# Five small re-orderings in a fused top-k attention and low-rank mixer kernel: parameters, one scratch tile, shares of products, and when two pairs add u

## The chip, the cores and the metric

The kernel runs on one core of a Trainium2 chip. The metric is device time in microseconds (us) of one execution. The engines are named as the profile names them: PE is TensorE (PEld its weight loads), DVE is VectorE, ACT is ScalarE, POOL is GpSimd, SP is SyncE, which here only issues DMAs. A "q" after a name (SPq, ACTq) is that engine's sequencer issuing a DMA.

## The reference, cut to what matters

```python
# attention: q, k, v of (8, 8, 576, 64)
scores = q @ k.T / sqrt(64)
kth = the 32nd largest score of each row
scores = where(scores >= kth, scores, -1e9)
x = softmax(scores) @ v                 # (8, 576, 512) after the heads are put side by side
# mixer: U (576, 32), V (32, 576), w_ch1 (512, 2048), w_ch2 (2048, 512)
h = x.T @ U @ V
u = x + h.T
out = u + relu(u @ w_ch1) @ w_ch2
```

All parameters U, V, w_ch1, w_ch2 arrive as 64-bit floats and are turned into 32-bit floats on the chip.

## The kernel before, in words

**Pairs and steps.** Heads are worked on two at a time: 8 batches of 4 pairs, so 32 pairs (`g`), numbered 0 to 31; batch b holds pairs 4b to 4b+3. A pair has 576 query rows for each of its two heads: four main tiles (`t` 0 to 3, 128 rows, both heads) and one tail tile (`t` 4, the last 64 rows of both heads). Steps (`n`) follow each other in a loop written out by hand. In the first four pairs every tile has a step of its own (20 steps, n 0 to 19). From pair 4 on a pair has four steps, and its last step works on tile 3 and the tail together: three rows of work, which the code calls lanes 0, 1 and 2, lane 2 being the tail. Pair 4 is steps 20 to 23, pair 5 steps 24 to 27, pair 6 steps 28 to 31, and so on.

**One tile's way.** `scores` (L350, the tail's at L382) puts scores in PSUM, ACT copies them to SBUF (L395; the tail's L415 and L418). `front` finds the 32nd largest score on DVE, by four rounds of MAX8 (L521, L539) and MATCH_REPLACE8 (L534); the tail's rounds write a scratch row, `place`, in the only buffer of the tag "tplace". From pair 5 on the main tiles are first folded to half their width: POOL adds the halves (L446), DVE takes their maximum (L448) and POOL subtracts (L449); DVE then takes the best of the lower half (L502, L500). Then ACT makes a "gap" tile for each lane (`least` L565, E L568: zero where the score is among the 32), POOL subtracts it from the scores (L569), and ACT takes the exponential (L453). The gap tiles have the tag "E", which has two buffers; a step with three lanes needs three. Then the weights are transposed: by PE (L631, L636) with copies by ACT (L632, L637) up to pair 5; from pair 6 on by DVE (L595) and DMAs to DRAM and back. `values` (L705, L708, tail L679) multiplies with v three steps after the tile's own step, and ACT copies the product to XT (L717, L686).

**u.** When a pair's tail has its values, `mixed` is put in the list `mixing`. From pair 4 on it first lets `lag` shares pass, then POOL scales XT (L737, L740), PE transposes it (L747, L758), and after the next tile's values PE multiplies with U (L770) and V (L782), ACT copies (L797), and POOL adds to make u (L798). XT and `scale` have one buffer each, so a pair's u must be done with them before the next pair's are written.

**Products.** With u of a whole batch there, `mlp(b)` makes its products on PE: first layer L842, second layer L859, in two parts of 320 and 256 columns, 256 products a batch; L854 and L870 are ACT's evictions, L871 POOL's addition of u. They run beside the attention of the next batch: `fill` is called eight times a step, and each call advances `mixing` once and issues one share of products. A unit of work is 512 columns; a full share is 1.02 units, in a step with two tiles 1.4 times that. For steps up to 38 (`n <= ALONE + BATCH + 2`) the share is multiplied by EARLY = 0.91, in steps 24 to 27 by SECOND = 0.84. The products of batch b+1 may not pass the fourth quarter of the contraction before batch b+1 has all its u (`whole`): a `fill` that meets this gate issues nothing and drops what was due. The last batch's products (`closing`, L935) come after all attention.

**Parameters.** There are 36 pieces of parameters in a fixed order (U, V, 16 of w_ch1, 16 of w_ch2). `next_params(1)` does three stages at once, on three different pieces: it issues the DMA of the next on SP (L157); for the one issued by the call before it sets up three ACT passes (L179, L180, L183), which the following `fill` calls issue one each; and for the one before that it issues the join: a shift on DVE (L202, for the last eight pieces L193) and two additions on POOL (L203, L205). In steps of pairs 0 to 3 it is called at two places, from pair 4 on in the middle of a step (L1328, pair 4 alone) and at its end (L1354).

The order on each engine is the order in which the code issues; each engine works its queue in that order.

Of the kernel before, what the change touches and what calls it, by code (L numbers as in the profile page):

```python
# [8 lines left out]
F32 = mybir.dt.float32  # L9
# [17 lines left out]
def kernel(  # L27
# [29 lines left out]
    B, H, S, D = q.shape  # L57
    P = 128
# [4 lines left out]
    NT, TAIL = 4, 64  # L63
# [3 lines left out]
    NPAIR = H // 2  # L67
# [3 lines left out]
    ALONE = NPAIR * CH  # L71
# [11 lines left out]
    attn = ctx.enter_context(tc.tile_pool(name="attn", bufs=2))  # L83
# [63 lines left out]
    def f64_raw(srcs):  # L147


        n, w = srcs[0].shape[0], srcs[0].shape[-1]  # L150
        raw = mlpp.tile([P, 2 * C], U32, tag="raw", name="raw", bufs=3)
        if len(srcs[0].shape) == 3:
            raw = raw.rearrange("p (f w) -> p f w", w=w)
        else:
            raw = raw[:, 0:w]
        for i, src in enumerate(srcs):
            nc.sync.dma_start(raw[i * n : (i + 1) * n], src)  # L157
        return raw[0 : len(srcs) * n]

    def f64_parts(raw, out):  # L160

        n, w = raw.shape[0], raw.shape[-1] // 2
        d = "p f" if len(raw.shape) == 3 else "p"
        low, hi = (raw.rearrange(f"{d} (w two) -> {d} w two", two=2)[..., i] for i in range(2))
        low8 = raw.bitcast(U8).rearrange(f"{d} (w eight) -> {d} w eight", eight=8)[..., 3]
        if out is None:
            if not spare:  # L170

                uT = mlpp.tile([P, NC, S], F32, tag="uT", name="uT")
                words = uT.rearrange("p c n -> p (c n)").bitcast(U32)
                spare.extend(words[:, i * SLAB : (i + 1) * SLAB] for i in range(NT))
            out = spare.pop()[0:n, 0:w]
        bits = out.bitcast(U32)
        lows, his = low.bitcast(F32), hi.bitcast(F32)
        passes.extend((
            lambda: nc.scalar.activation(bits.bitcast(F32), his, AF.Copy, scale=RESCALE),  # L179
            lambda: nc.scalar.activation(  # L180
                lows, low8, AF.Identity, bias=four[0:n], scale=-(1 + 2.0**-10) * 2.0**-26
            ),
            lambda: nc.scalar.activation(his, his, AF.Sign, bias=nudge[0:n]),  # L183
        ))
        return hi, bits, low, len(params) < LATE

    def f64_join(hi, bits, low, late, outs):

        if late:
            none = nought if len(bits.shape) == 2 else nought.rearrange("p o -> p o ()")
            nc.vector.scalar_tensor_tensor(  # L193
                out=bits,
                in0=bits,
                scalar=3,
                in1=none.to_broadcast(list(bits.shape)),
                op0=ALU.logical_shift_left,
                op1=ALU.bitwise_or,
            )  # L200
        else:
            nc.vector.tensor_single_scalar(bits, bits, 3, ALU.logical_shift_left)  # L202
        nc.gpsimd.tensor_tensor(bits, bits, hi, ALU.add)  # L203
        for dst, form in outs:
            nc.gpsimd.tensor_tensor(dst.bitcast(U32), form(bits), form(low), ALU.add)  # L205
# [26 lines left out]
    def next_params(n):  # L232

        while passes:
            passes.pop(0)()
        while parts:
            f64_join(*parts.pop(0))
        while raws:
            r, outs = raws.pop(0)
            if isinstance(outs, list):  # L240
                parts.append((*f64_parts(r, None), outs))
                continue
            made = f64_parts(r, outs)
            parts.append((*made, [(made[1], same)]))
        for _ in range(min(n, len(params))):
            srcs, outs = params.pop()
            raws.append((f64_raw(srcs), outs))
# [6 lines left out]
    def load(g):  # L254

        list(loading(g))
# [211 lines left out]
    def front(tiles):  # L468
# [5 lines left out]
        for g, t in tiles:  # L474
# [4 lines left out]
            n = S2.shape[1]  # L479
# [61 lines left out]
        for c, chunk, total, _, way in lanes:  # L541
            if way == "pooled":
                gap = attn.tile([P, S], F32, tag="E", name="E")
# [17 lines left out]
        if gaps:  # L561
            slots = [lane[0] for lane in gaps]
            lo, hi = min(slots), max(slots) + 1
            least = small.tile([P, 3], F32, tag="least", name="least", bufs=3)
            nc.scalar.mul(least[:, lo:hi], m8[:, lo:hi, 7], WIDEN)  # L565
            for c, chunk, *_ in gaps:
                gap = attn.tile([P, S], F32, tag="E", name="E")
                nc.scalar.activation(gap, chunk, AF.Relu, bias=least[:, c : c + 1], scale=-WIDEN)  # L568
                nc.gpsimd.tensor_tensor(chunk, chunk, gap, ALU.subtract)  # L569
            yield  # L570
# [585 lines left out]
    STEPS = len(steps)  # L1156
    BATCH = NPAIR * NT


    SLOTS, LONG, EARLY, SECOND = 8, 1.4, 0.91, 0.84  # L1160
    share = MLP_WORK / (NPAIR * SLOTS * (NT - 1 + LONG))
    fillers, mixing, due = [], [], 0.0

    def fill(k=1):


        nonlocal due
        for _ in range(k):
            if passes:
                passes.pop(0)()  # L1170
            if mixing and next(mixing[0], True):
                mixing.pop(0)
            part = share * (LONG if len(tiles(n)) > 1 else 1)
            if n <= ALONE + BATCH + 2:
                part *= SECOND if ALONE + NT <= n < ALONE + 2 * NT else EARLY
            due += part
            while due > 0:
                if not fillers:
                    due = 0.0
                    break  # L1180
                done = next(fillers[0], None)
                if done is None:
                    fillers.pop(0)
                elif not done:
                    due = 0.0
                else:
                    due -= done

    def tiles(n):

        return steps[n] if 0 <= n < STEPS else []

    def weighted(m):

        for g, t in tiles(m):
            values(g, t)
        if tiles(m)[-1][1] == NT:
            mixing.append(mixed(g, None, 1) if m < STEPS - 1 else mixed(g, 5, 0))

    def turn():  # L1200

# [6 lines left out]
            yield from turns(g, t)  # L1208

    load(0)  # L1210
    next_params(3)
    t = 0
    for _ in prep(0):
        pass
# [3 lines left out]
    for n in range(STEPS + 2):  # L1218
        if n < STEPS:
            g, t = steps[n][0]  # L1220
            if t == 0 and g < NPAIR:
                load(g + 1)
            if t == (1 if g < NPAIR else 2) and g + 1 < NP:
                ready = prep(g + 1)
            fronts[n] = front(steps[n])
            next(fronts[n])
            if owed:
                inverse(owed.pop(), 0, 2 * NT + 1)
        else:
            t = NT  # L1230
        here, last = fronts.get(n, iter(())), fronts.pop(n - 1, iter(()))
        if n >= ALONE - 1 and n <= ALONE:
# [12 lines left out]
            if n < ALONE:  # L1245
                split(*steps[n + 1][0])
                next(here)
                next(here)
                inverse(g, 0, 2 * NT)
                mixing.append(mixed(g, 1))  # L1250
                fill()
                next(here)
                continue
            fill()
            scores(*steps[n + 1][0])
            fold(*steps[n + 1][0])
            next(here)
            while mixing:
                fill()
# [44 lines left out]
        if ALONE <= n - 3 <= STEPS - 3:  # L1304
            weighted(n - 3)
            if waiting:
                waiting.clear()
                if next(mixing[0], True):
                    mixing.pop(0)
# [14 lines left out]
        if n < STEPS and n - 2 >= ALONE and len(tiles(n - 2)) > 1:  # L1324
            scale(steps[n - 2][0][0])
        next(here, None)
        if g == NPAIR and t < NT - 1:
            next_params(1)  # L1328
        fill()
        if n >= STEPS:  # L1330
            if n == STEPS:
                inverse(NP - 1, 0, 2 * NT + 1)
                scale(NP - 1)
            weighted(n - 2)
# [15 lines left out]
                coming = loading(g + 2) if g + 2 < NP else iter(())  # L1350
            next(coming, None)
        next(ready, None)
        if t != 0 or g == NPAIR + 1:
            next_params(1)  # L1354
        next(here, None)
        fill()
# [36 lines left out]
```

## Time and profile before

| what | value |
|---|---|
| median of 3 runs | 1661.03 us (1660.91 to 1661.57) |
| the profiled execution's own time | 1660.23 us |
| its span, first to last instruction | 1658.0 us |
| mean granted TensorE clock | 0.968 |
| PE busy | 1555.6 us (94%) |
| DVE busy | 1546.9 us (93%) |
| ACT busy | 992.0 us (60%) |
| POOL busy | 1009.4 us (61%) |
| PE's idle waits between 190 and 1560 us, the longest | 7.25 us, at 259.28 |

The page of the profile gives busy shares in 40 slices of 41.5 us, and groups of instructions by line. The views by stretch of time (windows) give each engine's busy time in a stretch; the views of waits name who waited for whom; the timeline lists instructions with the idle time before them in square brackets and what ended it. A busy PE is not PE at its peak, as the ends of pipelined matmuls are modelled; a fp32 product shows as two matmul records.

### The profile page before, as it was taken

How to read it: one execution, taken by the hardware profiler on the slowest of the kernel's cores; microseconds unless marked ns; L12 is line 12 of the kernel's file. 1: busy time of each engine (PE TensorE's matmuls, PEld its weight loads, DVE VectorE, ACT ScalarE, POOL GpSimd, SP SyncE). 2: the span in 40 equal slices, each digit the busy share in tenths (PEclk: the TensorE clock that was granted, in tenths of full speed). 3: DMA queues.
4: the chain of work that ended last, by engine and by line, in shares of the span. 5: the costliest groups of instructions: out<-in, count | busy, mean ns of one | idle time of the engine just before them, and what ended most of it. 6: DMA issues, size and time to landing. Idle time of an engine off the chain costs nothing.

```text
span 1658.0 us, 30248 instructions
## 1 busy us (share of the span) xinstructions
PE 1555.6 (94%) x9638; PEld 1182.7 (71%) x9638; DVE 1546.9 (93%) x4394; ACT 992.0 (60%) x2475; POOL 1009.4 (61%) x881
## 2 busy tenths in 40 slices
PE   4566698999999999999999999999999999999999
PEld 2344466787677877788777877788777877787776
DVE  7999998999999999999999999999999999994452
ACT  5888886665655566566655656565655656564320
POOL 4888756666656565656656565656666565653620
PEclk7787799999999999999999999999999999999999
DMA  4333321254445555454545455454545455543001
GB/s 113 98 101 99 86 76 25 57 133 135 126 130 137 133 154 133 131 139 130 134 125 141 128 154 133 134 137 131 133 126 141 128 151 134 136 123 109 7 2 28
DMA packets 280399, 189.42 MB, mean 114 GB/s; under 512 B 174288, under 2 KB 261168, under 8 KB 280240
## 3 DMA queue, kind: packets, MB, share of 16 engines
q1 hardware_dynamic: 259728, 117.62, 29.4%
q10 hardware_dynamic: 20512, 69.87, 13.1%
q8 instruction: 76, 1.25, 0.3%
q14 instruction: 83, 0.68, 0.1%
HBM read 116.49 MB, written 70.91 MB: 113 GB/s over the span
## 4 chain that ended last, share of the span: by engine, by line
PE 74%; DVE 19%; DMA 2%; POOL 1%; ACT 1%; issue 1%; SPq 1%; ACTq 0%; DVEq 0%; POOLq 0%
PE mm L859 23%; PE mm L842 22%; PE sc L350 7%; DVE m L539 7%; PE O L708 6%; DVE upper L534 6%; PE mm L935 3%; DVE first L521 2%; PE sc L382 2%; PE sc L935 2%; PE tp L935 2%; PE up L782 2%; PE O L705 1%; PE tp L631 1%; DMA PT<-away 1%
## 5 line engine op out<-in xcount | busy, mean ns | idle before, releaser
L842 PE MATMUL mm<-uT,w 128*128 128x320 f32 (+1 forms) x1792 | 463.3, 410 | 2.2 <-POOL uT L798 2.2
L859 PE MATMUL mm<-hT,w 128*128 128x320 f32 (+1 forms) x1792 | 460.2, 407 | 0.0
L569 POOL TENSOR_TENSOR Ssb<-Ssb,E 128x576 f32<-128x576 f32 x243 | 339.7, 1418 | 187.0 <-ACT E L568 187.0
L842 PEld LDWEIGHTS mm<-uT,w 128*128 128x128 f32 x1792 | 334.6, 191 | 102.0 <-issue 7.4
L859 PEld LDWEIGHTS mm<-hT,w 128*128 128x128 f32 x1792 | 332.0, 190 | 92.6 <-issue 10.2
L539 DVE MAX8 m<-upper 128x8 f32<-128x304 f32 (+1 forms) x774 | 362.3, 508 | 0.7
L534 DVE MATCH_REPLACE8 upper<-m,upper 128x304 f32<-128x304 f32 (+1 forms) x516 | 256.5, 504 | 0.0
L449 POOL TENSOR_TENSOR lower<-lower,upper 128x576 uint32<-128x576 uint32 x108 | 152.3, 1410 | 135.9 <-DVE upper L448 133.7
L446 POOL TENSOR_TENSOR lower<-Ssb 128x576 uint32<-128x576 uint32 x108 | 152.3, 1410 | 133.4 <-ACT Ssb L395 73.5
L453 ACT ACTIVATE Ssb<-Ssb,nmax 128x576 f32<-128x576 f32 x258 | 201.8, 784 | 15.7 <-POOL Ssb L545 7.8
L350 PE MATMUL sc<-qkT 64*128 64x288 f32 (+1 forms) x1056 | 177.2, 457 | 13.9 <-ACT Ssb L404 12.2
L568 ACT ACTIVATE E<-Ssb,least 128x576 f32<-128x576 f32 x243 | 176.2, 769 | 4.2
L502 DVE MAX8 upper<-lower 128x8 f32<-128x288 f32 x432 | 171.7, 438 | 2.7 <-POOL lower L449 2.7
L395 ACT COPY Ssb<-sc 128x576 f32<-128x576 f32 x216 | 127.6, 644 | 68.3 <-PE sc L350 68.1
L595 DVE STREAM_TRANSPOSE y<-Ssb 128x512 f32<-128x512 f32 (+1 forms) x312 | 154.0, 543 | 1.2 <-ACT Ssb L453 1.2
L708 PE MATMUL O<-PT,va 128*64 128x128 f32 x2048 | 143.7, 284 | 0.0
L854 ACT ACTIVATE hT<-mm 128x320 f32<-128x320 f32 (+1 forms) x224 | 91.2, 407 | 81.7 <-PE mm L842 78.7
L350 PEld LDWEIGHTS sc<-qkT 64*128 64x128 f32 (+1 forms) x1056 | 94.8, 195 | 54.7 <-issue 16.5
L708 PEld LDWEIGHTS O<-PT,va 128*64 128x64 f32 x2048 | 112.2, 139 | 16.2 <-issue 1.6
L534 DVE MATCH_REPLACE8 upper<-first,upper 128x304 f32<-128x304 f32 x216 | 97.4, 458 | 0.0
L500 DVE MATCH_REPLACE8 lower<-upper,lower 128x288 f32<-128x288 f32 x216 | 93.9, 442 | 0.0
L717 ACT COPY XT<-O 128x128 f32<-128x128 f32 x128 | 33.8, 264 | 98.3 <-PE O L708 94.0
(268 smaller groups left out, 2259.7 us busy)
## 6 DMA issues: line engine op xcount, KB each, us to landing
away<-y SPq DMA_DIRECT2D x416, 144.0 KB
PT<-away ACTq DMA_DIRECT2D x104, 576.0 KB
raw<-in_moe_w_ch_dram SPq DMA_DIRECT2D x32, 512.0 KB
va<-in_v_dram SPq DMA_DIRECT2D x64, 128.0 KB
scale<-rd ACTq DMA_DIRECT2D x56, 144.0 KB
out_dram<-ob SPq DMA_DIRECT2D x59, 128.0 KB
ld<-in_q_dram SPq DMA_DIRECT2D x108, 64.0 KB
ld<-in_k_dram SPq DMA_DIRECT2D x108, 64.0 KB
```

The lines of the kernel that those rows point to most:

```text
L350: nc.tensor.matmul(out, lhsT=qkT[half(h), 0, cols(t)], rhs=qkT[half(h), 1, lo:hi], start=True, stop=True,)
L446: nc.gpsimd.tensor_tensor(bottom, a.bitcast(U32), b.bitcast(U32), ALU.add)
L453: nc.scalar.activation(E, chunk, AF.Exp, bias=nmax, scale=SCALE, accum_out=total)
L502: nc.vector.max(spot, lower)
L534: nc.vector.match_replace(nxt, ms[c], curs[c], NEG)
L539: nc.vector.max(ms[c], curs[c])
L568: nc.scalar.activation(gap, chunk, AF.Relu, bias=least[:, c : c + 1], scale=-WIDEN)
L569: nc.gpsimd.tensor_tensor(chunk, chunk, gap, ALU.subtract)
L595: nc.vector.transpose(y[:, :, i * NT : i * NT + c].rearrange("p r c j -> p c r j"), E2[:, a : a + c * P].rearrange("p (c r j) -> p c r j", ...
L708: nc.tensor.matmul(O[half(h)], lhsT=va[:, h, j, :], rhs=PT[:, NT * h + j], start=False, stop=(j == NT - 1),)
L842: nc.tensor.matmul(phs[f][:, 0:w], lhsT=first_layer(cc, f), rhs=uT[:, cc, lo:hi], start=(cc == 0), stop=(cc == NC - 1),)
L859: nc.tensor.matmul(po[:, 0:w], lhsT=w2[:, f, c * P : (c + 1) * P], rhs=hTs[f][:, 0:w], start=(f == 0), stop=(f == NF - 1),)
```

## The change

1. Before the first step one piece of parameters is started instead of three. In pair 4 the call in the middle of a step is made in all its steps but the first, also in the last; the call at the end of a step is made from pair 4 on in steps with t < 3 instead of t > 0 or in pair 5. So the last three pieces are joined at the ends of steps 24, 25 and 26; before, at the ends of steps 22, 23 and 24.
2. The gap tile of lane 2, the tail's, is taken from the tag "tplace" instead of "E".
3. The factors of the shares are 1.1, 0.75, 0.91, 0.95 in pairs 4, 5, 6 and 7 (0.95 also in steps 36 to 38), instead of 0.91, 0.84, 0.91, 0.91 (0.91).
4. `mixed` of pairs 4 and 5 lets four shares pass instead of one before it scales XT.

```diff
             for c, chunk, *_ in gaps:
-                gap = attn.tile([P, S], F32, tag="E", name="E")
+                if c == 2:
+                    gap = attn.tile([P, S], F32, tag="tplace", name="E", bufs=1)
+                else:
+                    gap = attn.tile([P, S], F32, tag="E", name="E")
...
-    SLOTS, LONG, EARLY, SECOND = 8, 1.4, 0.91, 0.84
+    SLOTS, LONG, EARLY = 8, 1.4, (1.1, 0.75, 0.91, 0.95)
...
             if n <= ALONE + BATCH + 2:
-                part *= SECOND if ALONE + NT <= n < ALONE + 2 * NT else EARLY
+                part *= EARLY[min(max(n - ALONE, 0) // NT, NT - 1)]
...
-            mixing.append(mixed(g, None, 1) if m < STEPS - 1 else mixed(g, 5, 0))
+            mixing.append(mixed(g, None, 1 if g > NPAIR + 1 else 4) if m < STEPS - 1 else mixed(g, 5, 0))
...
-    next_params(3)
+    next_params(1)
...
-        if g == NPAIR and t < NT - 1:
+        if g == NPAIR:
             next_params(1)
...
-        if t != 0 or g == NPAIR + 1:
+        if t < NT - 1:
             next_params(1)
```

## The prediction

> **What bounds the kernel now.** I read the page's 40 slices first, then busy times by stretch, then the waits of DVE and PE between 230 and 520 us, then the timeline at each wait.
>
> ```profile
> PE   4566698999999999999999999999999999999999
> DVE  7999998999999999999999999999999999994452
> ```
> ```profile
> 12.00:235.00 223.00, 147.10 (x894) 97.42 (x891) 221.80 (x463) 183.05 (x432) 172.48 (x127) 0.79 0.33 95
> 235.00:335.00 100.00, 92.05 (x593) 67.79 (x591) 92.64 (x267) 65.05 (x162) 63.91 (x54) 0.97 0.20 48
> 335.00:431.00 96.00, 91.68 (x634) 73.98 (x632) 95.93 (x292) 59.01 (x150) 61.95 (x54) 1.00 0.52 137
> ```
>
> The columns are the stretch, its length, then busy us (and instructions) of PE, PEld, DVE, ACT, POOL, the granted clock, DMA share, GB/s. DVE is full from 12 us to about 1510 us, but for one place: in 235 to 335 it idles 7.4 us, in the 223 us before 1.2 us, in the 96 us after 0.1 us. So DVE sets the pace until attention ends, and only DVE time saved there counts. PE also reads full, but its busy time hides slack: in the batch at 805 to 991 us 256 products take 124.1 us at the chain's rates (16 records of 320 columns in 4.31 us, so 0.539 us a product; 0.431 us at 256 columns), and attention's PE work brings the sum to some 181 of 186 us (an estimate from the groups' rows). After 1510 us the last pair's way to u and the last batch's products are a fixed tail.
>
> ```profile
> DVE upper L448 <- ACT Stail L415: 3.4, 2, 2.5
> DVE upper L502 <- POOL lower L449: 1.9, 3, 1.0
> DVE y L595 <- ACT Ssb L453: 1.2, 2, 0.7
> DVE upper L448 <- ACT Ssb L395: 0.8, 1, 0.8
> ```
>
> These are DVE's waits in 230 to 520 us: total, count, longest. They are eight, 7.3 us, all between 260.34 and 329 us. Behind the first ones stands one PE stall:
>
> ```profile
> 253.28 1.29 POOL L203 TENSOR_TENSOR w<-w,raw 128x512 uint32<-128x512 uint32 x1 [3.28 <-DVE w L193]
> 255.88 2.77 POOL L569 TENSOR_TENSOR Ssb<-Ssb,E 128x576 f32<-128x576 f32 x2
> 257.32 0.78 ACT L568 ACTIVATE E<-Stail,least 128x576 f32<-128x576 f32 x1 [3.00 <-POOL Ssb L569]
> 259.28 1.11 PE L631 MATMUL tp<-ident,Ssb 128*128 128x128 f32 x4 [7.25 <-ACT XT L717]
> 281.70 0.76 DVE L448 TENSOR_TENSOR upper<-sc,Ssb 128x576 f32<-128x576 f32 x1 [2.52 <-ACT Stail L415]
> 286.42 0.82 DVE L502 MAX8 upper<-lower 128x8 f32<-128x288 f32 x2 [1.04 <-POOL lower L449]
> ```
>
> A parameter join holds POOL from 253.28 to 255.9; so its first subtraction is late; so the tail's gap waits for an E buffer (3.00 us on ACT); so the copy to XT behind it is late; so PE idles 7.25 us, runs late, and DVE waits for its scores at 281.70.
>
> **The change part by part.**
>
> *Tail's gap in the tail's row.* Its new wait, for the last MAX8 of `place`, is one that `least` before it makes already; the next tail's `place` comes 30 us later. ACT loses the 3.00 us wait at 257.32, and the L183 behind it (0.74 us) goes to another step: XT's copy ends at 255.5 to 256.2 instead of 259.2. In later batches this wait is 0.85 us on an ACT that is 60% busy: nothing.
>
> *Parameters.* DVE's 36 joins stay; the first stretch has no idle DVE to gain or lose. On SP, U's tail and V move behind the loads of pair 1, two pieces of w behind each later load: they are needed a pair or more later, so nothing. Without this cover ACT would wait as it does today at 25.34 us (8.7 us for V), where DVE loses nothing. What counts is pair 4's end: in step 23 the join moves from the end to the middle, where POOL idles 4.20 us before 248.58, so the hold at 253.28 goes. Two joins (DVE 0.65 to 1.16 us, POOL 2.57, ACT passes 2.2) move into steps 25 and 26. DVE does them where it now waits; the ACT passes stand ahead of the copies that DVE waits for: +0.5 (bounds 0 and 2.2).
>
> *Shares.* I counted products between values in both orders. By the values issued in step 24 the new kernel has issued 6.25 units more (5.4 us at 0.862 us a unit), in step 26 5.0, in steps 28 to 30 2.5, in step 37 4.5; then both stand at the gate at 147.75 units and are equal to the end. So no product work leaves the tail; the shares only choose where PE is late. PE's 5.4 us more fall into the 7.25 us stall: it reaches L631 at 256.3 to 256.9 instead of 252.0 and finds XT copied. If that cover failed, up to 5.4 us of PE would come on top. Net PE is 2.4 to 3.0 us earlier, 3.3 by the scores of step 26. Those of step 23 come 3.2 us later (7 products, 3.8 us, less 0.6 us that PE waited at 236.95), which DVE does not feel: today they are copied by 239.7 and used at 247.71.
>
> *u later.* In step 26 the scaling (1.44 + 0.71 us) leaves the way of L449, but the first output's L871 (0.87 us, after ACT's L870) takes its place there. In step 28 L798 (0.87 + 0.72) enters ahead of L449, where POOL comes straight from three subtractions and today makes DVE wait 0.35 us at 308.96. Pair 5's, in step 32, has 2 us and more of cover in DVE's transposes (L595).
>
> The sum, DVE wait by wait: 260.34, -0.8. 281.70, -2.2 (0.3 stays for ACT's order). 286.42, -0.7 (a join fills most). 308.96, +0.7 (1.59 of L798 for 0.87 of L871). 318.79, 320.04 and 321.44, -1.5 of 1.7: ACT then waited for PE, and L871 no longer stands before that L449. 328.74, -0.8. ACT passes, +0.5. Total **-4.8 us**. Against the profiled execution's 1660.23 that is 1655.4; the median stands 0.8 above it, so 1656.2.
>
> **What stands against it: PE's clock.** Equal at the gate means that PE has 4.5 units (3.9 us) less to do in 403 to 431 us, where it already waits. One such wait, today:
>
> ```profile
> 431.45 5.45 PE L842 MATMUL mm<-uT,w 128*128 128x320 f32 x12 [2.21 <-POOL uT L798]
> ```
>
> After 2.21 us idle, 12 records took 5.45 us, 0.454 each for 0.269, and the granted clock in 430 to 435 is 0.79. After 1.75 us idle at 403.11 it stayed 1.00. [...]
>
> **The rivals.**
>
> - *Half is given back* (1658.9). PE gains no lead, and u's join in step 28 decides: today in step 27 the second L798 ends 8.2 us after values began; from 302.01 that is 310.2, L449 ends at 311.6, and DVE, ready at 308.61, waits 3.0 instead of 0.35: +2.65 in place of +0.7. If L871 also holds L449 in step 26, the -0.7 is 0. Then -2.1. For it: POOL's chain there has no slack; against: PE leads by 3 us.
> - *All waits go* (1653.7). The whole 7.3 us. It needs POOL's L449 in steps 26 and 28 free, which the order speaks against.
> - *Slower: the clock falls at the gate* (1665.4). PE is busy some 25.6 us in 403 to 431; at 0.454 for 0.269 that is 17.7 more, less today's idle 2.8 and the 3.9 of products gone: 11.0 late. DVE's slack there is 1.85 us (ACT's copies end 817.64, L448 at 819.49, of the steady batch): DVE loses 9.2, less 4.8 gained: +4.4. It decides only if several waits of over 2 us follow each other; the single ones before 431 left the clock at 1.00.
> - *No effect at all* would need the stall at 259.28 to stay; DVE's last MAX8 ends at 252.6 and ACT is idle then, so I count it within the first rival.
>
> **How the numbers follow.** Forecast 1656.2 (own range 1654.2 to 1658.2): 0.55. Half given back: 0.27. All waits go: 0.10. The clock: 0.08. The range of 8 in 10 leaves out the clock and the end of the fastest case: 1653.2 to 1661.0, where the upper end also takes the 2.2 us of ACT passes on top of the first rival. A measurement of this kernel tells about 0.2% (3.3 us) from no change, so faster means under 1657.7: 0.50 of the forecast's cases and the 0.10. Faster 0.60, same 0.32, slower 0.08.
>
> **What would show it.** Right: no ACT wait before the tail's E; the PE stall near 259 under 2 us with the clock at 1.00 after it; DVE's busy time in 235 to 335 us at 96 to 98; the wait at L448 in step 26 under 0.5; a wait of about 1 us at L502 in step 28; from 435 us the same program, some 5 us earlier. Wrong: DVE waits for scores in steps 21 to 24 (the extra products not covered), L502 in step 28 waiting 2 us or more, a granted clock under 0.9 over 400 to 440, or DVE waits after 435 us.

## The result, and the profile after

| | before | after |
|---|---|---|
| median of the runs beside each other | 1660.97 us (6 runs, 1660.19 to 1661.57) | 1655.19 us (6 runs, 1653.33 to 1655.75) |
| the profiled execution: time, span | 1660.23, 1658.0 us | 1655.26, 1653.4 us |
| mean granted clock | 0.968 | 0.971 |

The ratio is 0.9964, 95% interval 0.9951 to 0.9977: faster by 5.8 us, a third of a percent. In the changed file lines behind L567 stand three further down: E is L571, the subtraction L572, the first transposes L634, values L708, XT's copy L720, products L845 and L862, u L801, the output's addition L874, DVE's transposes L598.

Busy time by stretch, after (the columns as in the prediction):

```profile
12.00:235.00 223.00, 147.54 (x898) 98.13 (x899) 221.83 (x464) 179.76 (x427) 167.39 (x124) 0.80 0.32 92
235.00:335.00 100.00, 97.97 (x641) 72.66 (x640) 97.57 (x286) 71.70 (x178) 73.25 (x61) 1.00 0.27 66
335.00:431.00 96.00, 90.50 (x599) 71.86 (x598) 95.93 (x291) 56.69 (x146) 59.13 (x53) 0.98 0.49 131
```

DVE's idle time from 235 to 335 us is down from 7.4 to 2.4 us, and the granted clock there is 1.00 instead of 0.97. DVE's waits in 230 to 520 us, after:

```profile
DVE upper L502 <- POOL lower L449: 1.6, 2, 0.9
DVE upper L448 <- ACT Stail L415: 1.4, 1, 1.4
DVE y L598 <- ACT Ssb L453: 0.4, 1, 0.4
```

Four waits for eight; two of them, of 0.70 and 0.38 us, are new and lie at 502 and 512 us. The place of the old PE stall, in the timeline after:

```profile
252.10 2.78 POOL L572 TENSOR_TENSOR Ssb<-Ssb,E 128x576 f32<-128x576 f32 x2 [3.80 <-ACT E L571]
...
252.60 0.76 ACT L571 ACTIVATE E<-Stail,least 128x576 f32<-128x576 f32 x1
...
253.26 0.24 ACT L720 COPY XT<-O 128x128 f32<-128x128 f32 x1
...
253.69 0.60 PE L634 MATMUL tp<-ident,Ssb 128*128 128x128 f32 x4
```

No join stands ahead of POOL's subtraction, ACT makes the tail's E with no wait, XT is copied at 253.3 instead of 259.0, and PE passes by. And DVE's steps 28 and 30, after:

```profile
303.86 0.82 DVE L502 MAX8 upper<-lower 128x8 f32<-128x288 f32 x2 [0.93 <-POOL lower L449]
...
322.08 0.76 DVE L448 TENSOR_TENSOR upper<-sc,Ssb 128x576 f32<-128x576 f32 x1 [1.44 <-ACT Stail L415]
```

Where the time went is best read from one line that DVE runs 108 times in the same order in both kernels, L448, by its start after less its start before:

| L448, number (us before) | 1 (248) | 4 (282) | 8 (329) | 21 (483) | 29 (576) | 53 (855) | 108 (1491) |
|---|---|---|---|---|---|---|---|
| after less before, us | -1.63 | -5.67 | -6.66 | -6.66 | -5.35 | -4.45 | -4.38 |

So 6.66 us are won by step 30, held up to 483 us, and 2.3 us of them are given back later. Not all of the 6.66 us is the edits': 0.5 us of it is there at the first MAX8 (11.20 and 10.69 us), which in the 14 profiles of this document starts at 10.65 to 11.26 us under the old order of the parameters and at 10.69 to 11.19 us under the new one. Up to number 8, DVE's waits from 12 us on fell by 4.9 us (7.29 to 2.36), that start gave 0.5, and the joins' DVE instructions were 0.4 shorter (20.9 to 20.5 us in all; 19.6 to 21.5 us over the 14 profiles); some 0.8 us lie in many records of a few hundredths.

### The profile page after: what moved, and what is told of

Read it like the earlier page. It is cut to its first block, busy times and chain, and to the rows that moved or that the text cites. A ratio compares the mean times of both kernels' runs of the same rounds, so it can differ in the third digit from the quotient of the medians.

```text
span 1653.4 us, 30246 instructions
## 1 busy us (share of the span) xinstructions
PE 1554.9 (94%) x9638; PEld 1182.0 (71%) x9638; DVE 1546.1 (94%) x4394; ACT 990.1 (60%) x2475; POOL 1009.4 (61%) x881
## 3 DMA queue, kind: packets, MB, share of 16 engines
q8 instruction: 76, 1.25, 0.3%
## 4 chain that ended last, share of the span: by engine, by line
PE 69%; DVE 22%; DMA 3%; POOL 2%; SPq 1%; ACT 1%; issue 1%; DVEq 0%; ACTq 0%; POOLq 0%
PE mm L862 21%; PE mm L845 20%; DVE m L539 7%; PE sc L350 6%; DVE upper L534 6%; PE O L711 6%; PE mm L938 3%; DVE first L521 2%; PE tp L938 2%; PE sc L938 2%; PE sc L382 2%; PE up L785 2%; DVE y L598 1%; PE O L708 1%; DVE upper L502 1%; DVE place L534 1%
## 5 line engine op out<-in xcount | busy, mean ns | idle before, releaser
L845 PE MATMUL mm<-uT,w 128*128 128x320 f32 (+1 forms) x1792 | 460.2, 408 | 2.1 <-POOL uT L801 2.1
L862 PE MATMUL mm<-hT,w 128*128 128x320 f32 (+1 forms) x1792 | 460.4, 407 | 0.0
L572 POOL TENSOR_TENSOR Ssb<-Ssb,E 128x576 f32<-128x576 f32 x243 | 339.7, 1417 | 196.9 <-ACT E L571 196.8
L845 PEld LDWEIGHTS mm<-uT,w 128*128 128x128 f32 x1792 | 333.3, 190 | 102.2 <-issue 10.0
L862 PEld LDWEIGHTS mm<-hT,w 128*128 128x128 f32 x1792 | 331.9, 190 | 91.7 <-issue 9.8
L449 POOL TENSOR_TENSOR lower<-lower,upper 128x576 uint32<-128x576 uint32 x108 | 152.3, 1410 | 123.6 <-DVE upper L448 119.7
L453 ACT ACTIVATE Ssb<-Ssb,nmax 128x576 f32<-128x576 f32 x258 | 201.8, 784 | 19.9 <-POOL Ssb L545 9.6
L571 ACT ACTIVATE E<-Ssb,least 128x576 f32<-128x576 f32 x243 | 176.2, 768 | 4.2
L598 DVE STREAM_TRANSPOSE y<-Ssb 128x512 f32<-128x512 f32 (+1 forms) x312 | 154.0, 544 | 0.4 <-ACT Ssb L453 0.4
L720 ACT COPY XT<-O 128x128 f32<-128x128 f32 x128 | 33.8, 264 | 114.3 <-PE O L711 107.3
```

Source lines behind the costliest of these rows:

```text
L453: nc.scalar.activation(E, chunk, AF.Exp, bias=nmax, scale=SCALE, accum_out=total)
L598: nc.vector.transpose(y[:, :, i * NT : i * NT + c].rearrange("p r c j -> p c r j"), E2[:, a : a + c * P].rearrange("p (c r j) -> p c r j", ...
L845: nc.tensor.matmul(phs[f][:, 0:w], lhsT=first_layer(cc, f), rhs=uT[:, cc, lo:hi], start=(cc == 0), stop=(cc == NC - 1),)
L862: nc.tensor.matmul(po[:, 0:w], lhsT=w2[:, f, c * P : (c + 1) * P], rhs=hTs[f][:, 0:w], start=(f == 0), stop=(f == NF - 1),)
```

## The experiments

All runs are against the unchanged kernel on the same chip. An interval is some 0.1% wide to each side, 1.6 us, so differences between two variants of under 2 us rest on their profiles, one of each variant, and on the times of single executions where these do not overlap. A column of the next two tables gives L448 number 21 (483 us before) less that of before, with the difference of the first MAX8 taken out: it shows what a variant has won before anything happens after 490 us. As the joins' time varies by 1 us and more between profiles, less than that is not to be read from it.

### Each edit alone

```diff
 # gap alone: before +
+                if c == 2: gap = attn.tile([P, S], F32, tag="tplace", name="E", bufs=1)
 # parameters alone: before +
-    next_params(3)
+    next_params(1)     # and the two calls' conditions in the loop
 # shares alone: before +
+    EARLY = (1.1, 0.75, 0.91, 0.95)
 # later u alone: before +
+    mixed(g, None, 1 if g > NPAIR + 1 else 4)
```

Expected of the gap's tile alone:

> The kernel before with the tail's gap in the tail's row alone. Theory (one PE stall near 259 us starts DVE's waits): ACT's 3.00 us wait before the tail's E goes, POOL's hold by the join stays; XT's copy about 3 us earlier, the 7.25 us PE stall at about 4.2, DVE's waits at 260.34 and 281.70 gone or nearly, 286.42 kept: 1658 (-2.5 to -3.3). Rival (POOL's hold by the join alone starts it): within 0.5 us of before. Rival (each of the four edits brings its own quarter): -1.4.

Expected of the parameters alone:

> The kernel before with the parameters' calls alone. Theory: POOL's hold at 253.28 goes, so its first subtraction starts some 2.3 us earlier, the E buffer comes free by 255.1 and the L183 pass is not ahead of the copy; PE stall down to about 4 us or less, as with the gap alone: -2.5 to -3.5 us. The two edits are then substitutes, and their singles sum to more than both together. Rival: the two joins moved into steps 25 and 26 cost as much as they free, within 0.5 us of before. Rival of quarters: -1.4.

Expected of the shares alone:

> The kernel before with the shares alone. Theory: PE reaches the stall near 259 us some 5 us later and still leaves it at about 259.3 (the copy to XT is ACT's), but without a fall of the clock behind it and with 1 to 3 units less to do until the scores of steps 26 and 30: stall under 3 us, wait at 281.70 down by 2 us or more: -2 to -3 us. Rival (the shares only push scores back in steps 21 to 23): +1 to +5 us. Rival of quarters: -1.4.

Expected of the later u alone:

> The kernel before with the later u of pairs 4 and 5 alone. Theory: the wait at 286.42 goes (-1.0), but with PE as late as it is now the second L798 of step 28 holds L449 and the wait at 308.96 grows from 0.35 to 2 or 3 us: +0.5 to +2 us over before. Rival: L449 is free in step 26 and PE early enough in step 28: -1.0. Rival of quarters: -1.4.

| alone | median (before 1660.59) | ratio, 95% interval | PE's stall near 257 | DVE's waits, 230 to 340 | L448 number 21 |
|---|---|---|---|---|---|
| gap | 1657.58 | 0.9981, 0.9972 to 0.9990 | 4.13 | 4.89 | -2.05 |
| parameters | 1656.76 | 0.9977, 0.9968 to 0.9986 | 5.57 | 4.51 | -2.59 |
| shares | 1659.18 | 0.9990, 0.9981 to 0.9998 | 2.20 | 7.41 | -0.99 |
| later u | 1661.57 | 1.0006, 0.9998 to 1.0015 | 6.53 | 8.67 | +0.32 |

The gap's tile and the parameters each win most of the gain, 3.0 and 3.8 us. The timeline of the gap's tile alone shows how:

```profile
252.68 1.29 POOL L203 TENSOR_TENSOR w<-w,raw 128x512 uint32<-128x512 uint32 x1 [3.27 <-DVE w L193]
253.64 0.76 ACT L571 ACTIVATE E<-Stail,least 128x576 f32<-128x576 f32 x1
...
255.26 0.25 ACT L720 COPY XT<-O 128x128 f32<-128x128 f32 x1
255.30 2.78 POOL L572 TENSOR_TENSOR Ssb<-Ssb,E 128x576 f32<-128x576 f32 x2
```

The join still holds POOL up to 255.3, but ACT no longer needs POOL. With the parameters alone it is the other way round:

```profile
253.07 2.77 POOL L569 TENSOR_TENSOR Ssb<-Ssb,E 128x576 f32<-128x576 f32 x2 [3.80 <-ACT E L568]
254.50 0.78 ACT L568 ACTIVATE E<-Stail,least 128x576 f32<-128x576 f32 x1 [0.85 <-POOL Ssb L569]
255.50 0.26 ACT L717 COPY XT<-O 128x128 f32<-128x128 f32 x1
```

Here ACT still waits for an E buffer, but 0.85 us where it was 3.00, as POOL is not held. Both bring the copy to 255.3 or 255.5: they are two ways to the same thing. With the parameters alone the stall is 5.57 us, where I had expected 4 or less: it ends 3.5 us earlier than before, but PE also reaches it 1.8 us earlier (250.24 for 252.03).

The shares alone missed what I expected. PE did fill the stall with products, but nothing brought XT earlier, so PE's stall only became shorter and the scores were late all the same:

```profile
258.15 0.65 PE L631 MATMUL tp<-ident,Ssb 128*128 128x128 f32 x4 [2.20 <-ACT XT L717]
...
281.17 0.76 DVE L448 TENSOR_TENSOR upper<-sc,Ssb 128x576 f32<-128x576 f32 x1 [2.55 <-ACT Stail L415]
286.72 0.82 DVE L502 MAX8 upper<-lower 128x8 f32<-128x288 f32 x2 [1.86 <-POOL lower L449]
```

PE starts L631 only 1.1 us earlier than before, its clock is 0.68 over the five us from 258 on, and DVE waits at the same two places, 7.41 us up to 340 us against 7.29 before. So its 1.4 us is not in these waits; where it comes from stays open, and at number 21 it is no more than the joins' time varies.

The later u alone clears the way of L449 in step 26 (no wait at 286) and closes it in step 28. Its POOL timeline:

```profile
305.81 0.88 POOL L798 TENSOR_TENSOR uT<-uT,scale 128x320 f32<-128x320 f32 x1
307.40 0.73 POOL L798 TENSOR_TENSOR uT<-uT,scale 128x256 f32<-128x256 f32 x1 [0.71 <-ACT scale L797]
308.09 1.41 POOL L449 TENSOR_TENSOR lower<-lower,upper 128x576 uint32<-128x576 uint32 x1
```

and DVE waits for that L449:

```profile
309.53 0.82 DVE L502 MAX8 upper<-lower 128x8 f32<-128x288 f32 x2 [2.63 <-POOL lower L449]
```

That is the rival "half is given back", with 2.63 us for its 3.0: the wait is real when PE has no lead, and the other edits keep it down to 0.93. The later u's own 1.0 us over before is within the interval.

### Each edit left out

The edits are the same, undone one at a time in the changed kernel.

Without the gap's tile:

> The new kernel with the tail's gap back in E. Theory: POOL is free at 253, so the third gap waits about 0.9 us as in every later batch, and PE arrives there late enough: within 0.7 us of the new kernel (1655.2 to 1656). Rival (the gap's row carries the gain): 2 us or more slower than the new kernel.

Without the parameters' change:

> The new kernel with the parameters' calls of before. Theory: the join holds POOL at 253 for 2.6 us, but the tail's gap doesn't need an E buffer; the exponentials come 2 us later, the PE stall is 1 to 2 us: 0.5 to 1.5 us slower than the new kernel. Rival (the parameters carry the gain): 2 us or more slower.

Without the shares:

> The new kernel with the shares of before. Theory: the stall has lost its first 3 us to the other edits but PE arrives at 252 and idles some 3 to 4 us, with a fall of the clock; PE is 1 to 2 us later at the scores of step 26 and does more in steps 24 to 30: 1 to 2.5 us slower than the new kernel. Rival (the shares don't matter, as both stand equal at the gate): within 0.5 us.

Without the later u:

> The new kernel with the u of pairs 4 and 5 one share after the values, as before. Theory: the wait at L502 in step 28 falls from 0.93 to about 0.3 or nothing, the one in step 26 comes back with 0.3 to 1.0: within 0.7 us of the new kernel. Rival (the later u is a real part of the gain): 1 us or more slower.

| left out | median (before 1660.91) | ratio, 95% interval | DVE's waits, 230 to 340 | 340 to 1500 | L448 number 21 |
|---|---|---|---|---|---|
| gap | 1656.76 | 0.9975, 0.9964 to 0.9985 | 3.70 | 2.06 | -3.90 |
| parameters | 1656.18 | 0.9969, 0.9959 to 0.9980 | 2.36 | 3.32 | -5.78 |
| shares | 1655.81 | 0.9972, 0.9962 to 0.9982 | 4.16 | 2.32 | -4.41 |
| later u | 1653.77 | 0.9956, 0.9943 to 0.9968 | 2.31 | 1.74 | -6.33 |
| none (the changed kernel) | 1655.19 (before 1660.97) | 0.9964, 0.9951 to 0.9977 | 2.36 | 3.24 | -6.15 |

Leaving out either of the first two costs 1.0 to 1.6 us in the medians, where each alone won 3.0 to 3.8. At the stall they replace each other: counted from L448 number 1, XT's copy starts at 11.25 us before, at 8.15 with the gap's tile alone, at 8.46 with the parameters alone, and at 7.51 with both (the row without the shares). The sum of the times does not show this: alone the four add up to 7.3 us of gain and together they give 5.8, but up to number 21 they add up to 5.3 alone and give 6.15 together. What the changed kernel lacks in the end it lost after 490 us.

The rows differ from what I expected. Without the parameters' change DVE's waits are those of the changed kernel, and the 1.0 us by which its last L448 is later is there at number 1 already, 0.57 of it at the first MAX8. So beside the other three edits the profiles show no gain of the parameters' change. Without the shares the stall (4.13 us at 253.60) and the fall of the clock behind it (0.66 over the next five us) are back, as expected; that costs 1.7 us at number 21, though only 0.6 in the medians. Without the gap's tile the cost is not "within 0.7" but 2.2 us at number 21. The stall near 254 stays away, but the third gap waits for an E buffer in step 27 too:

```profile
298.64 0.78 ACT L568 ACTIVATE E<-Stail,least 128x576 f32<-128x576 f32 x1 [0.85 <-POOL Ssb L569]
...
299.62 0.66 PE L631 MATMUL tp<-ident,Ssb 128*128 128x128 f32 x4 [1.83 <-ACT XT L717]
```

In the changed kernel the tail's E has no wait there, and PE waits less, and earlier:

```profile
296.88 0.66 PE L634 MATMUL tp<-ident,Ssb 128*128 128x128 f32 x4 [0.85 <-ACT XT L720]
```

PE goes on 2.74 us later without the gap's tile (0.5 of it from the start), has the same 48 product records to do until the tail's scores of step 30, and L448 number 8 is 2.74 us later.

What I had not expected either is the fourth row: without the later u the kernel is faster, by 1.4 us in the medians. Its five executions (1652.89 to 1654.08) lie below five of the six of the changed kernel (1655.08 to 1655.75; the sixth is 1653.33). DVE's waits up to 340 us are the same, only elsewhere (1.30 us at 282, 0.54 at 322 and 0.48 at 327, in place of 0.93 at 304 and 1.44 at 322). The difference lies after 490 us: at number 21 the two stand within 0.2 us, the start taken out.

### What happens after 490 us

In the changed kernel PE waits for the weights of one tile there, and then:

```profile
491.10 0.49 PE L708 MATMUL O<-PT,vd 128*128 128x128 f32 x2 [1.85 <-DMA PT<-away]
...
492.75 2.29 PE L350 MATMUL sc<-qkT 64*128 64x288 f32 x8
```

Without the later u the same place reads:

```profile
491.03 0.49 PE L708 MATMUL O<-PT,vd 128*128 128x128 f32 x2 [1.07 <-DMA PT<-away]
...
492.47 1.24 PE L350 MATMUL sc<-qkT 64*128 64x288 f32 x8
```

The same eight score records took 2.29 us and 1.24 us. Three further runs test this, the wait at 322 and the one at 304, each by one small edit of the changed kernel:

```diff
 # less early
-    SLOTS, LONG, EARLY = 8, 1.4, (1.1, 0.75, 0.91, 0.95)
+    SLOTS, LONG, EARLY = 8, 1.4, (1.1, 0.75, 0.85, 0.98)
 # two products earlier (n is the step)
+            part *= {44: 1.13, 45: 0.87}.get(n, 1)
 # u behind L449: pair 4, after the copy to Tb
-        yield
+        for _ in range(5 if g == NPAIR else 1):
+            yield
```

Less early:

> Third and fourth factor 0.85 and 0.98 instead of 0.91 and 0.95; by the values issued in step 30 PE has 2.4 to 3.2 products (1.3 to 1.7 us at 0.539 us) less behind it, and at the gate the same. Theory (in the changed kernel PE's extra products make the scores of step 30 late): DVE's wait of 1.44 us near 322 falls under 0.3, L448 from then to 490 us starts 1.1 to 1.4 us earlier than in the changed kernel, time about 1654.2. Rival (PE, not DVE, sets the end after 490 us): the wait at 322 goes, but the last L448 is at most 0.4 us earlier, time 1655.2. Second rival (ACT's order makes the tail's copy late): the wait stays above 1 us.

Two products earlier:

> Two products (1.08 us) are moved from behind to ahead of the values that wait at 491 us; nothing else moves. Theory (PE's 1.85 us of idle time lowers its clock, and this makes the scores late that DVE and POOL then wait for): PE waits 0.7 to 0.9 us there, the granted clock of 490 to 495 is over 0.95, the 8 score records take 1.24 us instead of 2.29, DVE's waits at 502 (0.70) and 512 (0.38) go, time 1653.8 to 1654.3. Rival (those waits come from POOL's order, the clock has no part): scores take 1.24 us, but the waits stay within 0.2 us, time 1655.2.

u behind L449:

> Pair 4's u is joined four shares later still, so that both L801 of step 28 stand behind L449. Theory (L801 ahead of L449 makes DVE's wait of 0.93 us at 303.9, but PE then sets the pace at 322): the wait at 303.9 goes, the one at 322 grows from 1.44 to 2.0 to 2.4, time 1655.2 within 0.5. Rival (the 0.93 is the price of the later u in the time): the wait goes, the one at 322 stays at 1.4, time 1654.3.

| changed kernel and | median (before 1660.68) | ratio, 95% interval | wait at 304 | at 322 | PE's wait at 491 | DVE's waits, 340 to 1500 |
|---|---|---|---|---|---|---|
| less early | 1653.88 | 0.9961, 0.9948 to 0.9975 | 0.94 | 0.89 | 1.50 | 1.88 |
| two products earlier | 1653.47 | 0.9956, 0.9944 to 0.9969 | 0.93 | 1.43 | none | 1.31 |
| u behind L449 | 1654.29 | 0.9962, 0.9949 to 0.9974 | none | 1.61 | 1.47 | 1.85 |

*Two products earlier* fits its theory, though PE has no idle time left where I had expected 0.7 to 0.9 us of it, and the time is a little under the range. PE's clock is 1.00, and the waits at 502 and 512 are gone. Changed kernel:

```profile
490.00:495.00 5.00, 3.90 (x27) 2.42 (x27) 4.96 (x17) 2.55 (x5) 2.79 (x3) 0.73 0.57 138
495.00:500.00 5.00, 5.00 (x25) 3.85 (x24) 5.00 (x18) 3.88 (x11) 1.41 (x1) 0.93 0.45 89
```

With the two products earlier:

```profile
490.00:495.00 5.00, 5.00 (x41) 3.67 (x40) 4.97 (x18) 4.10 (x11) 3.49 (x4) 1.00 0.65 149
```

Its median is 1.7 us under the changed kernel's (1.4 with each set against its own runs of before), its profiled execution 2.1 us; none of its times is over 1654.04. Up to 483 us its L448 stands where the changed kernel's stands (within the 0.2 us by which the two started apart), so all of the difference comes after: 1.3 us by L448 number 25, with the waits at 502 and 512, and 0.5 more at number 36, with the wait for the tail's scores at 649; the rest lies in the later waits. The clock rival of the prediction is thus real in kind, at a wait that it did not name, and costs DVE 1.3 us at once and 1.8 by number 36, where I had reckoned 9.2.

That it is the clock, and not PE's idle time itself, shows in *less early*, where the products before 491 us stay where they were:

```profile
491.02 0.49 PE L708 MATMUL O<-PT,vd 128*128 128x128 f32 x2 [1.50 <-DMA PT<-away]
...
492.47 1.24 PE L350 MATMUL sc<-qkT 64*128 64x288 f32 x8
```

PE goes on within 0.1 us of the changed kernel's time, after 1.50 us idle for 1.85, but its clock stays at 1.00, the scores take 1.24 us, and DVE has no wait at 502 or 512. All 14 profiles agree. In nine PE waits 1.02 to 1.55 us at this place, in three 0.33 or not at all, and in these twelve the clock stays at 1.00 and DVE has neither wait. In two, the changed kernel (1.85 us) and the one without the parameters' change (2.63 us), the clock falls (0.66 over the next five us in both), and both waits are there (0.70 and 0.38 us; 0.70 and 0.37).

*Less early* was half right. The wait at 322 went to 0.89 and not to under 0.3. I had counted products from the start; but PE waits once more at 297, for XT (0.85 us), and only what is issued between there and the scores of step 30 counts. There it was one product less (46 records for 48), 0.54 us, and the wait fell by 0.55. Its time came out near the 1654.2 of its theory by luck: at 490 us its L448 is 0.06 us ahead of the changed kernel's and not 1.1 to 1.4, and the 1.65 us by which the last one is ahead come after, as the clock did not fall at 491.

*u behind L449* took the wait at 304 away, as both readings said, and L448 number 8 stood within 0.15 us of the changed kernel's: the wait moved to 322 (1.61, not the 2.0 to 2.4 expected) and to two waits on L453 at 312 and 313. So the 0.93 us of L801 ahead of L449 cost nothing by itself; PE's scores in step 30 set the pace there. Its median is 0.9 us lower all the same (0.6 against its own runs of before); in its profile PE's wait at 491 is 1.47 us and the clock stays at 1.00.

### A version of all that

```diff
 # the changed kernel +
+        for _ in range(5 if g == NPAIR else 1):
+            yield
...
+            part *= {29: 0.7, 32: 1.15, 33: 1.15, 44: 1.13, 45: 0.87}.get(n, 1)
```

> The changed kernel with what the last three runs gave: pair 4's u four shares later still, three products (1.6 us) of step 29 moved behind the scores of step 30, and the two products moved ahead of the values at 491 us. Theory (DVE sets the pace up to some 830 us, and PE only where its clock falls): no DVE wait over 0.5 us from 230 to 340, none at 502 and 512, PE waits under 1.5 us at 491 with the clock over 0.95; L448 at 461 us stands 2.0 to 2.4 us ahead of the changed kernel's, time 1651.0 to 1652.0. Rival (PE's own work bounds a batch, so what DVE gains by 340 is waited for later): L448 at 461 us is 2 us ahead, but the waits on the tail's copy from 640 us on add 1 us or more, and the time is 1652.8 to 1653.5, the time of the run with the two products moved alone.

Median 1652.84 us (before 1660.34), ratio 0.9959, interval 0.9946 to 0.9973: the lowest median of all, but not distinct from that of the two products alone. DVE's waits in 230 to 520 us are nearly gone:

```profile
DVE y L598 <- ACT Ssb L453: 0.4, 2, 0.2
DVE upper L502 <- POOL lower L449: 0.3, 1, 0.3
DVE upper L448 <- ACT Stail L415: 0.2, 1, 0.2
```

That settles the wait at 322: three products moved out of the way (42 records for 48 between the wait for XT at 297 and the tail's scores) leave 0.20 us of the 1.61 with u behind L449 alone. But the lead was smaller than expected, and it did not last. Ahead of the changed kernel, L448 stood 1.25 us at number 8 and 0.78 at 461 us, where both readings had said 2 or more. Ahead of the run with the two products it stood 1.0 us at 461 us and 0.25 us at its end. What takes it back, in 520 to 1480 us of this kernel:

```profile
DVE upper L448 <- ACT Stail L415: 1.2, 4, 0.4
```

These are waits for the tail's scores, one in each later batch. The time from one L448 to the one 16 later (one batch, from number 12 on), worked out from the starts:

| us a batch | 1st | 2nd | 3rd | 4th | 5th | 6th |
|---|---|---|---|---|---|---|
| before | 185.87 | 185.85 | 185.85 | 185.94 | 186.32 | 186.37 |
| after | 187.17 | 186.37 | 186.22 | 186.24 | 186.23 | 186.24 |
| two products earlier | 185.84 | 185.87 | 185.85 | 185.99 | 186.21 | 186.26 |
| this version | 185.87 | 185.87 | 186.35 | 186.23 | 186.26 | 186.22 |

A batch takes 185.85 us where DVE sets the pace and 186.23 where it waits once for PE. Before, and in the run with the two products, DVE's pace held for over three batches; in this version, whose DVE is 1 us further ahead, PE's takes over in the third. A lead of DVE is used up at 0.38 us a batch. So what this rival said of the time happened (1652.84), and the theory's 1651.0 to 1652.0 was not reached. The waits on the tail's copy add up to 1.24 us after 640 us, 0.67 more than in the run with the two products.

## Why the prediction was right, point by point

**The total.** It forecast -4.8 us, the profiled execution shows -4.97 (1660.23 to 1655.26), the medians -5.8. Up to step 30 the waits fell as the sum says. That the total is as near is in part luck: two things that were not in the sum nearly cancel, 1.7 us won by an earlier start and shorter DVE work, and 2.3 us given back after 490 us.

**The chain behind the stall** held at every link: join, subtraction, E buffer, copy to XT, PE. Each of the two edits that cut it alone moved XT's copy from 259.0 to about 255.4. But the prediction priced the gap's tile in step 23 alone, and put the 0.85 us that ACT waits for E later at nothing. In step 27 it is not nothing: without the gap's tile PE's wait for XT there is 1.83 us instead of 0.85.

**The terms.** DVE's waits in 12 to 340 us, forecast and measured change:

| wait | forecast | measured |
|---|---|---|
| 260.34 | -0.8 | -0.80 |
| 281.70 | -2.2 | -2.52 |
| 286.42 | -0.7 | -1.04 |
| 308.96, u's join ahead of L449 | +0.7 | +0.58 |
| 318.79, 320.04, 321.44 | -1.5 | -1.70 |
| 328.74 | -0.8 | +0.56 |
| ACT passes | +0.5 | none seen |
| sum | -4.8 | -4.92 |

The mis-sized term is the wait at 328.74, which I struck out and which grew from 0.88 to 1.44. What failed there is "PE leads by 3 us": a lead gained at 259 is not carried to step 30, since PE waits for XT once more at 297 and starts from there; the last kernel's three products show what decided instead. The 0.3 us left for ACT's order and the 0.5 us for ACT's passes were not seen.

**"From 435 us the same program, some 5 us earlier"** failed. It was 6.66 us earlier at 483 and 4.4 at the end. The first differs by the 0.5 us of the start and 1.2 us of slightly shorter DVE work that I had put at nothing; the second by the fall of the clock at 491 us and the waits for the tail's scores after it, which I had put at nothing. "DVE waits after 435 us" stood in my own list of signs of being wrong, and it came: DVE waits 3.24 us from 340 to 1500 us, 1.31 before.

**The clock.** I took a fall to matter only after several waits of over 2 us in a row at 403 to 431 and reckoned that DVE would lose 9.2 us by it. One wait of 1.85 us at 491, outside that stretch, was followed by a fall (0.66 over the next five us), and 1.8 to 2.1 us were lost. The forecast's sum counts nothing for the clock; no run shows that PE's waits leave it alone: after 9 of the 14 idle times of 2.2 to 2.7 us in the profiles it fell. My own list of signs named the clock only over 400 to 440. There it was 0.96 on the mean, and 0.72 in 415 to 420, with no harm to DVE.

**u later.** The mechanism and the place were right, the sign in company was not shown by them: its +0.7 at step 28 costs nothing once PE sets the pace at 322, and its saving at 286 is lost in the same way. That the kernel is faster without it shows in the single times; in the profiles the difference is that the clock does not fall at 491, where PE idles 1.07 us and not 1.85. That the shorter idle time is the reason is not shown, as the clock also stayed at 1.00 after 1.50 and 1.55 us there. Why the products stand 0.7 us later there without the later u was not settled: PE's order was compared only by the products ahead of each tile's values, where it is the same, and the two profiles also differ by a fall of the clock at 425 (0.66 over five us without the later u, 1.00 with it).

**The shares.** I had PE's extra products fill the stall and gave them no gain of their own; alone they are worth 1.4 us, in company 0.6, which is within the interval. The profiles show a gain in company: without them the stall of 4.13 us is back, and L448 number 21 is 1.7 us later.

## What to carry to other kernels

When a stall is removed, follow the engine that was late to its next wait on the bounding engine's chain: it starts anew there, and only the work issued between that wait and its own delivery decides what comes next (here 48, 46 and 42 records between PE's wait at 297 and the tail's scores, and waits of DVE for these scores of 1.44, 0.89 and 0.20 us). Two edits that cut one chain at two links are not added. To compare variants that differ by so little, follow one repeated instruction through the profile, and stop before a fall of the clock that only some profiles have (two of 14 at 491 us). And where two engines need nearly the same time for a round (185.85 and 186.23 us here), a lead of the first is a loan: ask how many rounds are left to eat it.

## What the runs showed of the hardware

In these profiles the length of an idle time of PE does not decide alone whether the clock falls after it; a longer one is followed by a fall more often. I took all idle times of PE of at least 1.0 us between 235 and 1500 us in the 14 profiles, and the mean granted clock of the 5 us after each; a fall shows as 0.5 to 0.7, no fall as 1.00:

| idle, us | idle times | falls |
|---|---|---|
| 1.0 to 1.6 | 27 | 3 |
| 1.6 to 2.1 | 9 | 3 |
| 2.2 to 2.7 | 14 | 9 |
| over 4 | 5 | 5 |

One of the three falls in the first row, after 1.28 us, came while the clock was still down from another.

One wait, PE's for u at the gate (424 to 431 us), is 2.21 to 2.26 us long in 12 of the 14 profiles; the clock fell after it in seven and stayed at 1.00 in five. Changed kernel with u behind L449:

```profile
420.00:431.00 11.00, 8.48 (x35) 5.47 (x36) 11.00 (x34) 5.07 (x13) 4.60 (x6) 1.00 0.52 146
```

with less early products:

```profile
420.00:431.00 11.00, 8.69 (x30) 5.55 (x31) 11.00 (x34) 5.17 (x13) 4.62 (x5) 0.84 0.44 130
```

PE's wait in these was 2.25 and 2.26 us. What decides between the two outcomes of one and the same wait is not shown. Nor do the profiles show one length below which the clock stays and above which it falls: in the changed kernel the clock was 0.66 over the five us after an idle time of 1.39 us, at 416.74, and 1.00 after one of 2.06 us, at 424.79. What a fall costs depends on where it lies: the one at 491 us went with some 2 us of 1655, while the falls near 425 cost nothing that DVE's waits show (no profile has one of 0.15 us or more between 340 and 500 us). The times of one and the same kernel can stand in two groups (less early: 1652.88, 1653.07 and 1653.88, then 1655.40 and 1655.96). Only one execution of each kernel has a profile, so that the two groups come from the fall at 491 us is an inference.
